# A gated-attention and two-MLP kernel: phase rounded by an int32 write, first weights decoded in x's buffers, SyncE's first transfers in a fixed order, a new plan of steps, last stores split

## The chip, the cores and the metric

The kernel runs on one core of one Trainium2 chip. The metric is device time in microseconds (us) from the start to the end of one execution; less is better. The profile's span, from the first to the last instruction, is a little shorter than that time.

## What is computed

Attention with a complex decay per step, then two MLPs over 3072 tokens (4 batches of 768) with 384 features and 2048 hidden units, all in float32:

```python
mag = sqrt(a_re**2 + a_im**2); scale = minimum(mag, 0.999) / (mag + 1e-6)
for t in range(S):                      # S_re, S_im: [B, H, 48, 48]
    S_re, S_im = a_t * (S_re + 1j * S_im)   # real and imaginary part, a_t scaled
    S_re += outer(k_t, v_t)
    y_t = q_t @ S_re
x = y.reshape(3072, 384)
h = x @ moe_w_in;  x = (h * clip(h + 3, 0, 6) / 6) @ moe_w_out
h = x @ moe2_w_in; out = (h * sigmoid(1.702 * h)) @ moe2_w_out
```

## The kernel before

The recurrence is done in 24 chunks of 128 steps. A preparation block covers 256 tokens (two chunks). For each block the decays' logarithms and angles are summed along time (two scans), and q and k are multiplied by exp, cos and sin of the sums. Only block 0 is split in two halves of one chunk each; its steps carry a third number (`round.0.1` is half 1 of block 0). Rows of q and k are then put into another partition order by small transfers from SBUF to SBUF, the "repack": `repE.c`/`reqE.c` move the cos part of chunk `c` and `repS.c`/`reqS.c` the sin part; `rep` is issued by SyncE (SP) and GpSimd (POOL), `req` by ScalarE (ACT), and `req` exists in block 0 alone. One chunk of attention on TensorE (PE) is `sc` (scores), `kt` (k transposed), `pv`, `ud` (state update) and, in chunks 0 to 3, `xp`; ACT copies `ks` and `ysb`, and VectorE (DVE) does the mask `p` and the state `um`/`ua`.

The result x of a chunk is split into a high and a low part, `xh` (ACT) and `xl` (DVE), since a float32 product is made of three fast matmuls: high*high, low*high, high*low. The first MLP is cut into slots; `in.s` is the first matrix of slot s, `g1` to `g4` its gate on ACT, DVE, ACT, DVE, and `out.s` its second matrix. In the first two blocks of 512 tokens the slots `in.0` to `in.3` do tokens 0 to 255 with the weights wi0 to wi3, `in.4` to `in.7` tokens 256 to 511 with the same. Each of these is 18 matmuls of 256 columns.

The 16 weight pieces of the first MLP (even: wi, odd: wo, two of a number) come as 768 KB each of packed words. `W.i` loads one, DVE decodes it in three steps `da`, `db`, `dc`, ACT makes the high part (`hi.i`) and DVE the low part (`lo.i`). Before, the decoded words go to two buffers of a pool `st`.

The order of DVE, ACT and PE in the first MLP and the attention is written out in the string `PLAN`, a list of such steps made by a planner; each engine runs its steps in that order and waits on semaphores. SP's and POOL's order is left to the scheduler. Matmuls `wm.0` (16 of them, without use for the result) stand ahead of the first chunk. After the plan (slot 82 on) a loop over the remaining slots follows, with the second MLP.

Of the kernel before, what the change touches and what calls it, by code (L numbers as in the profile page):

```python
# [43 lines left out]
cos.0.1 qksin.0.0 reqE.0 qkcos.0.1 repS.0 reqS.0 qksin.0.1 W.5 da.3 La.1 reqE.1 repS.1 da.4 db.3 reqS.1 repE.1 db.4 kt0.0 dc.3 sc0.0 W.6 ks0.0 W.7 dc.4 tab1.1
kt1.0 sc1.0 p0.0 ks1.0 hi.3 ud.0 p1.0 lo.3 im2.1 pv0.0 um.0 pv1.0 re2.1 da.1 ysb.0 mag2.1 Lq.1 sc0.1 hi.4 W.9 kt0.1 ln.1 p0.1 sc1.1 lo.4 ks0.1 pv0.1 inv.1 p1.1
mag.1 kt1.1 db.1 pv1.1 ks1.1 half.1 eps.1 xp.0 dc.1 ysb.1 lneps.1 ud.1 da.2 lnhalf.1 decay.1 xp.1 xh.0 scan.1 invhalf.1 xh.1 tan.1 E0.1 xl.0 E1.1 xl.1 lastE.1
ua.1 lastqk.1 in.0 tab2.1 qkE.1 atan.1 um.1 in.2 hi.1 La.2 carry.1 low.1 Lv.2 angle.1 g1.0 W.11 W.10 W.12 g1.2 W.13 round.1 W.8 turns.1 frac.1 lo.1 abs.1 db.2
sin.1 cos.1 keep.1 dc.2 qkcos.1 hi.2 re2.2 tab1.2 qksin.1 repE.2 im2.2 lo.2 W.14 repS.2 g2.0 in.1 mag2.2 g3.0 g4.0 ln.2 g2.2 W.15 out.0 inv.2 Lv.4 da.8 Lv.3
g1.1 db.8 repS.3 eps.2 g2.1 dc.8 mag.2 g3.1 da.5 repE.3 half.2 hi.8 sc0.2 lneps.2 g4.1 kt0.2 g3.2 p0.2 sc1.2 ks0.2 lo.8 lnhalf.2 kt1.2 p1.2 pv0.2 ks1.2 decay.2
invhalf.2 pv1.2 g4.2 ud.2 scan.2 ysb.2 Lq.2 xp.2 ua.2 E0.2 low.2 um.2 sc0.3 xh.2 db.5 E1.2 kt0.3 sc1.3 p0.3 ks0.3 xl.2 kt1.3 lastE.2 p1.3 lastqk.2 pv0.3 ks1.3  # L50
dc.5 tab2.2 pv1.3 da.6 tan.2 ud.3 ysb.3 hi.5 db.6 xp.3 atan.2 lo.5 carry.2 out.1 dc.6 xh.3 xl.3 hi.6 da.7 angle.2 in.4 lo.6 round.2 g1.4 in.3 db.7 turns.2 dc.7
out.2 g1.3 ua.3 hi.7 g2.3 frac.2 g3.3 in.7 g4.3 abs.2 g2.4 sin.2 lo.7 cos.2 qkE.2 out.3 g3.4 g1.7 g4.4 tab1.3 in.6 qkcos.2 keep.2 repE.4 qksin.2 out.4 g1.6
g2.6 da.12 in.5 g3.6 g2.7 g4.6 g3.7 db.12 in.9 g1.5 g4.7 g2.5 dc.12 g3.5 in.8 g4.5 hi.12 um.3 g1.9 lo.12 repS.5 out.5 g1.8 da.14 da.9 db.14 repS.4 out.6 db.9
dc.14 La.3 dc.9 hi.14 repE.5 out.7 lo.14 hi.9 lo.9 g2.8 sc0.4 g2.9 g3.8 kt0.4 g3.9 p0.4 sc1.4 ks0.4 g4.8 im2.3 kt1.4 p1.4 pv0.4 ks1.4 g4.9 re2.3 pv1.4 da.10
da.11 ud.4 db.10 ysb.4 xf.4 mag2.3 sc0.5 dc.10 ln.3 sc1.5 ua.4 Lq.3 hi.10 in.12 p0.5 Lv.5 inv.3 um.4 Lv.6 mag.3 db.11 out.8 eps.3 p1.5 lo.10 g1.12 lneps.3
dc.11 in.10 da.13 hi.11 g2.12 xh.4 db.13 in.11 g1.10 lo.11 g3.12 g2.10 dc.13 g3.10 out.9 g1.11 g4.10 hi.13 g2.11 pv0.5 decay.3 g3.11 half.3 out.10 g4.11
lnhalf.3 g4.12 invhalf.3 pv1.5 lo.13 scan.3 out.11 ysb.5 xf.5 tan.3 E0.3 in.13 low.3 E1.3 xl.4 da.15 lastE.3 lastqk.3 qkE.3 tab2.3 out.12 atan.3 db.15 g1.13
in.15 La.4 angle.3 xh.5 g2.13 in.14 round.3 g3.13 turns.3 g1.15 g4.13 g1.14 frac.3 out.13 xl.5 abs.3 g2.14 sin.3 g2.15 in.16 cos.3 dc.15 keep.3 g3.14 qkcos.3
g3.15 in.17 hi.15 qksin.3 repE.6 im2.4 tab1.4 in.18 g4.14 repS.6 g1.16 g4.15 lo.15 g1.17 g1.18 clip.4 out.14 repS.7 g2.16 re2.4 g2.17 g3.16 mag2.4 out.15
# [793 lines left out]
```

## Time and profile before

| | |
|---|---|
| three runs of before | 996.52, 997.92, 1000.21 us (median 997.92) |
| profiled execution | 998.55 us, span 996.8 us |
| PE busy | 948.4 us (95% of the span), mean granted clock 0.983 |
| DVE, ACT, POOL busy | 643.9, 517.7, 105.8 us |
| chain that ended last | PE 89%, DVE 5%, ACT 2%, DMA 2% |

PE is busy in almost all of the span, and the busy share of the other engines is an average over a crowded start and a quieter rest. So what matters is the time at which PE waits, and the time that it runs at the lower of its two clocks (1.2 GHz, shown as 0.50; 1.00 is 2.4 GHz).

### The profile page before, as it was taken

The page shows a single profiled execution, that of the slowest core. Times are in us where ns is not written, and L with a number is a line of the kernel's source. Part 1 is how long each engine was busy: PE and PEld are TensorE (multiplying, and loading weights), DVE is VectorE, ACT ScalarE, POOL GpSimd, SP SyncE. Part 2 cuts the span into 40 slices and gives each one's busy share as a digit, 9 for nine tenths or more (in the row PEclk, how much of TensorE's full clock was granted, in tenths as well). Part 3 has the DMA queues.
Part 4 walks back from the last instruction along what each step waited for, and adds up shares of the span by engine and source line. Part 5 has one row for each costly group of instructions (what it writes and reads, how often), then busy time and mean ns, then how long its engine had stood idle before and what let it go on. Part 6 is the DMA issues. An engine that isn't in the chain of part 4 may idle for free.

```text
span 996.8 us, 14418 instructions
## 1 busy us (share of the span) xinstructions
PE 948.4 (95%) x5378; PEld 804.8 (81%) x5378; DVE 643.9 (65%) x919; ACT 517.7 (52%) x860; POOL 105.8 (11%) x218
## 2 busy tenths in 40 slices
...
GB/s 270 283 163 196 66 49 125 131 128 128 122 118 96 72 120 128 80 97 73 72 132 240 159 151 40 1 125 128 127 190 127 158 159 127 111 1 1 32 1 35
DMA packets 70684, 113.63 MB, mean 114 GB/s; under 512 B 9936, under 2 KB 55632, under 8 KB 70608
## 3 DMA queue, kind: packets, MB, share of 16 engines
...
q10 hardware_dynamic: 384, 0.26, 0.1%
...
## 4 chain that ended last, share of the span: by engine, by line
PE 89%; DVE 5%; ACT 2%; DMA 2%; issue 1%; SPq 0%; POOL 0%; ACTq 0%; DVEq 0%
PE h L634 38%; PE o L672 38%; PE sc L517 4%; PE ud L563 3%; PE yps L537 3%; PE yps L539 2%; PE kt L526 1%; DMA wr<-in_w1i 1%; DMA QK<-qk 1%; DVE qk L474 1%; DVE pE L473 1%; DMA xf<-ysb 0%; DVE wi L389 0%; DVE pA L436 0%; DVE wx L127 0%
## 5 line engine op out<-in xcount | busy, mean ns | idle before, releaser
L634 PE MATMUL h<-xh,wi 128*128 128x512 f32 (+1 forms) x1248 | 364.9, 376 | 10.8 <-ACT wi L380 6.4
L672 PE MATMUL o<-gh,wo 128*128 128x512 f32 (+1 forms) x1248 | 364.2, 376 | 0.1
L634 PEld LDWEIGHTS h<-xh,wi 128*128 128x128 f32 x1248 | 228.0, 190 | 52.9 <-ACT wi L380 6.6
L672 PEld LDWEIGHTS o<-gh,wo 128*128 128x128 f32 x1248 | 227.2, 189 | 41.7 <-issue 0.9
L634 PE MATMUL h<-xl,wi 128*128 128x512 f32 (+1 forms) x624 | 233.9, 375 | 0.5 <-DVE xl L606 0.4
L672 PE MATMUL o<-gl,wo 128*128 128x512 f32 (+1 forms) x624 | 233.1, 374 | 0.0
L659 DVE TENSOR_TENSOR gl<-tt,gh 128x512 fp32r<-128x512 f32 x192 | 132.2, 690 | 84.0 <-ACT gh L654 83.7
L654 ACT ACTIVATE gh<-tt 128x512 fp32r<-128x512 f32 x192 | 121.0, 632 | 109.3 <-DVE tt L649 65.2
L649 DVE TENSOR_TENSOR tt<-tt,h 128x512 f32<-128x512 f32 x96 | 66.0, 688 | 144.8 <-ACT tt L641 144.8
L641 ACT ACTIVATE tt<-h 128x512 f32<-128x512 f32 x96 | 57.4, 598 | 172.2 <-PE h L634 167.2
L634 PEld LDWEIGHTS h<-xl,wi 128*128 128x128 f32 x624 | 118.3, 190 | 22.2 <-DVE xl L606 1.2
L672 PEld LDWEIGHTS o<-gl,wo 128*128 128x128 f32 x624 | 117.8, 189 | 21.0
L639 ACT ACTIVATE tt<-h,b 128x512 f32<-128x512 f32 x96 | 65.7, 685 | 75.5 <-PE h L634 72.1
L647 DVE SCALAR_TENSOR_TENSOR tt<-tt,h 128x512 f32<-128x512 f32 x96 | 65.2, 683 | 42.4 <-ACT tt L639 42.2
L551 POOL DMA_DIRECT2D xf<-ysb x60 | 30.9, 521 | 242.0 <-ACT ysb L543 232.1
L517 PE MATMUL sc<-QK 96*128 96x128 f32 x384 | 55.0, 291 | 0.0
L517 PEld LDWEIGHTS sc<-QK 96*128 96x128 f32 x384 | 50.8, 203 | 2.2 <-issue 0.7
L486 POOL DMA_DIRECT2D QK<-pE x70 | 35.7, 515 | 157.8 <-DVE pE L473 95.9
L521 DVE TENSOR_TENSOR p<-sc,causal 128x512 f32<-128x512 f32 x48 | 33.0, 688 | 20.7 <-PE sc L517 19.7
L537 PE MATMUL yps<-p,v 128*48 128x128 f32 (+1 forms) x384 | 40.4, 291 | 0.1
L486 POOL DMA_DIRECT2D QK<-qk x70 | 36.4, 526 | 15.6 <-issue 5.8
L603 ACT ACTIVATE xh<-xf 128x384 fp32r<-128x384 f32 x44 | 22.8, 518 | 27.8 <-DMA xf<-ysb 11.5
(111 smaller groups left out, 877.9 us busy)
## 6 DMA issues: line engine op xcount, KB each, us to landing
...
```

The source lines that it names most:

```text
L486: e.dma_start(out=dst, in_=src)
L517: T.matmul(out=sc[:, i, :], lhsT=kv_(4 * g + i), rhs=qv(4 * g + i), start=True, stop=True)
L521: V.tensor_tensor(out=p, in0=s_["sc", g], in1=causal.unsqueeze(1).to_broadcast([P, 4, CH]), op=ALU.mult)
L537: T.matmul(out=yps[r0:r1, h // 2, :], lhsT=v_c[c][:, e], rhs=s_["p", g][:, i, :], start=True, stop=first)
L634: T.matmul(out=h[:, i, :], lhsT=w[:, k, :], rhs=x[:, k, :], start=(k == 0 and q == 0), stop=(k == 2 and q == 2))
L639: A.activation(out=t, in_=ht[s], func=AF.Relu, bias=b3)
L641: A.activation(out=t, in_=ht[s], func=AF.Sigmoid, scale=1.702)
L647: V.scalar_tensor_tensor(out=t, in0=t, scalar=6.0, in1=ht[s], op0=ALU.min, op1=ALU.mult)
L649: V.tensor_tensor(out=t, in0=t, in1=ht[s], op=ALU.mult)
L654: A.activation(out=hi, in_=gt[s][0], func=AF.Copy)
L659: tail[:] = [V.tensor_tensor(out=lo, in0=gt[s][0], in1=gt[s][1], op=ALU.subtract)]
L672: T.matmul(out=acc[:, o:o + n], lhsT=w[:, e * P:e * P + P], rhs=g[:, i, :], start=(f == o == q == 0), stop=(f == FT - 1 and q == 2), skip_ ...
```

## The change

The diff, with most of the plan's lines left out:

```diff
-MAGIC = 12582912.0
...
 PLAN = """
...
-inv.0.1 db.0 lneps.0.0 eps.0.1 decay.0.0 mag.0.1 lneps.0.1 half.0.1 lnhalf.0.0 decay.0.1 lnhalf.0.1 scan.0.0 invhalf.0.0 invhalf.0.1 scan.0.1 E0.0.0 E1.0.0
...
+hi.1 kt1.0 W.5 dc.2 W.9 ks1.0 W.4 ysb.0 lo.1 ud.0 W.15 ln.1 lo.0 inv.1 xp.0 um.0 mag.1 eps.1 half.1 da.3 lneps.1 lnhalf.1 decay.1 reqS.1 scan.1 invhalf.1 xh.0
...
+    first_sp = {"last": None, "open": True}
+
+    def sp(**kw):
+
+        r = nc.sync.dma_start(**kw)
+        if first_sp["last"] is not None:
+            after(r, first_sp["last"])
+        if first_sp["open"]:
+            first_sp["last"] = r
...
-        nc.sync.dma_start(out=raw[i].rearrange("p n w -> p (n w)"), in_=(w1i, w1o)[kind][j].bitcast(U32))
+        sp(out=raw[i].rearrange("p n w -> p (n w)"), in_=(w1i, w1o)[kind][j].bitcast(U32))
...
         if k == 0:
-            w32[i] = st.tile([P, 768], U32, tag="ws", name="wx")
+            if i >= 4:
+                w32[i] = st.tile([P, 768], U32, tag="ws", name="wx")
+            else:
+                if i % 2 == 0:
+                    memo["wx"] = xp.tile([P, 2, 768], U32, tag=("xl", "xh")[i // 2], name="wx")
+                w32[i] = memo["wx"][:, i % 2]
...
-            o, n = (0, TB) if c is None else (c * CH, CH)
-            nc.sync.dma_start(out=ins[b, "a"].rearrange("p q j t -> p (q j) t")[:, :, o:o + n],
-                              in_=a_t[b].rearrange("p (q j t) -> p (q j) t", q=2, j=3)[:, :, o:o + n])
+            src = a_t[b].rearrange("p (q j t) -> p q j t", q=2, j=3)
+            if c is None:
+                sp(out=ins[b, "a"], in_=src)
+            else:
+                for q in (1, 0):
+                    (nc.scalar.dma_start if c == 0 and q else sp)(out=ins[b, "a"][:, q, :, c * CH:c * CH + CH], in_=src[:, q, :, c * CH:c * CH + CH])
...
-        op("round", lambda: V.tensor_scalar(out=pB(), in0=pA(), scalar1=2.0 / TURN, scalar2=MAGIC, op0=ALU.mult, op1=ALU.add))
-        op("turns", lambda: V.tensor_scalar(out=pB(), in0=pB(), scalar1=MAGIC, scalar2=None, op0=ALU.subtract))
-        op("frac", lambda: V.scalar_tensor_tensor(out=pA(), in0=pA(), scalar=2.0 / TURN, in1=pB(), op0=ALU.mult, op1=ALU.subtract))
+        whole = lambda: pB().bitcast(mybir.dt.int32)
+        op("round", lambda: V.tensor_scalar(out=whole(), in0=pA(), scalar1=2.0 / TURN, scalar2=None, op0=ALU.mult))
+        op("frac", lambda: V.scalar_tensor_tensor(out=pA(), in0=pA(), scalar=2.0 / TURN, in1=whole(), op0=ALU.mult, op1=ALU.subtract))
...
-                e = (nc.sync, nc.gpsimd, nc.scalar)[i % (3 if b == 0 else 2)]
-                if e in queues:
-                    e.dma_start(out=dst, in_=src)
+                q = "SASGGA"[i] if b == 0 else "SG"[i % 2]
+                if q in queues:
+                    {"S": sp, "G": nc.gpsimd.dma_start, "A": nc.scalar.dma_start}[q](out=dst, in_=src)
+            if c == 1 and y == 1 and "S" in queues:
+                first_sp["open"] = False
...
+        if m == 1 and b == NT // TK - 1 and e:
+            for i in range(2):
+                part = slice(i * TB, i * TB + TB)
+                if e == 1 or i:
+                    V.tensor_copy(out=y[:, part], in_=ops_["o"][e][:, part])
+                else:
+                    A.activation(out=y[:, part], in_=ops_["o"][e][:, part], func=AF.Copy)
+                (nc.sync, nc.scalar)[i].dma_start(out=out[b * 2 + i, :, e, :], in_=y[:, part])
+            return
```

So one DVE instruction (`turns`) is gone from each block; the weights 0 to 3 are decoded in two buffers that x's parts use only later; SP's transfers up to chunk 1's repack keep the order in which they are written; a chunk's repack in block 0 gives ACT one of the two large pieces (48 partitions x 774), which was POOL's; the first quarter of the decays comes through ACT's queue; and the last two output tiles are copied and stored in halves. Three places show how the plan moved the rest.

SP at the start, before. `a` are decays (142 is block 0, 274 block 1), `wr` weights, `QK_249` and `QK_276` chunks 0 and 1 of the repack:

```order
L399 DMA a_142<-in_a_t 128x6x128 x2
L412 DMA v_146<-in_v_t 128x384
L360 DMA wr_148<-in_w1i 128x1536
L406 DMA qk_150<-in_qk_t 128x3x128 x4
L412 DMA v_155<-in_v_t 128x384
L360 DMA wr_157<-in_w1o 128x1536
L360 DMA wr_159<-in_w1o 128x1536
L360 DMA wr_161<-in_w1i 128x1536
L360 DMA wr_165<-in_w1i 128x1536
L360 DMA wr_270<-in_w1o 128x1536
L486 DMA QK_249<-pE_197 48x774
L486 DMA QK_249<-pE_197 16x258
```

SP at the start, of the change, from chunk 0's weights on (chunk 1 is now `QK_281`, block 1's decays `a_220`):

```order
L326 DMA wr_159<-in_w1o 128x1536
L326 DMA v_162<-in_v_t 128x384
L326 DMA wr_164<-in_w1i 128x1536
L326 DMA v_169<-in_v_t 128x384
L326 DMA a_220<-in_a_t 128x1536
L326 DMA QK_249<-pE_196 48x774
L326 DMA QK_249<-pE_196 32x258
L326 DMA QK_249<-qk_150 48x774
L326 DMA QK_249<-qk_150 32x258
L326 DMA QK_281<-pE_196 48x774
L326 DMA QK_281<-pE_196 32x258
L326 DMA QK_281<-qk_150 48x774
```

Three weights instead of six stand ahead of the repacks, and block 1's decays, which stood between the two parts of chunk 0's repack (row 13 of SP before), now stand ahead of it too.

ACT around chunk 1's repack, before (all of it follows chunk 0's at once):

```order
L486 DMA QK_249<-qk_150 32x258 x2
L486 DMA QK_276<-pE_197 32x258 x2
L486 DMA QK_276<-qk_150 32x258 x2
L531 ACTIVATE ks_306<-kt_293 128x384
L325 ACT_TABLE_LOAD
L531 ACTIVATE ks_306<-kt_312 128x384
```

ACT at the same place, of the change:

```order
L502 DMA QK_281<-pE_196 48x774
L502 DMA QK_281<-pE_196 32x258
L549 ACTIVATE ks_317<-kt_301 128x384
L393 ACTIVATE wo0_321<-wx_167 128x768
L549 ACTIVATE ks_317<-kt_323 128x384
L561 ACTIVATE ysb_336<-yps_117 112x512
L339 ACTIVATE pB_286<-pA_269 128x768
L339 ACTIVATE pA_269<-pB_286 128x768
L339 ACTIVATE pC_360<-pB_286 128x768
L344 ACTIVATE pA_269<-pA_269,bone_109 128x768
L339 ACTIVATE pA_269<-pA_269 128x768
L339 ACTIVATE a_220<-a_220 128x768
```

Behind the last of these stands `QK_281<-qk_150 48x774`, ACT's part of chunk 1's sin repack: ten activations have moved in between ACT's cos part and its sin part.

DVE ahead of the first gate, before (`wi1_537` is the low part of the weights of `in.1`, `tt_512` the first gate):

```order
L465 SCALAR_TENSOR_TENSOR pA_351<-pA_351,pB_339 128x768
L389 TENSOR_TENSOR wo0_503<-wx_353,wo0_503 128x768
L125 SCALAR_TENSOR_TENSOR wx_436<-wr_161,wx_436 128x768
L466 TENSOR_SCALAR carry_111<-pA_351 128x3
L127 SCALAR_TENSOR_TENSOR wx_436<-wr_161,wx_436 128x768
L473 TENSOR_TENSOR pE_452<-qk_358,pB_339 128x12x128
L474 TENSOR_TENSOR qk_358<-qk_358,pC_399 128x12x128
L389 TENSOR_TENSOR wi1_537<-wx_436,wi1_537 128x768
L647 SCALAR_TENSOR_TENSOR tt_512<-tt_512,h_460 128x512
```

DVE of the change, from the two low parts of the weights to x's low part of chunk 1 (`xl_373<-xp_465`):

```order
L402 TENSOR_TENSOR wi2_443<-wx_392,wi2_443 128x768
L123 SCALAR_TENSOR_TENSOR wx_213<-wr_319,wx_213 128x768
L486 TENSOR_TENSOR qk_387<-qk_387,pE_380 128x12x128
L121 TENSOR_SCALAR wx_473<-wr_418 128x768
L123 SCALAR_TENSOR_TENSOR wx_473<-wr_418,wx_473 128x768
L477 TENSOR_TENSOR pB_286<-pB_286,carry_111 128x3
L452 SCALAR_TENSOR_TENSOR pA_269<-mask_p_107,pB_286 128x768
L480 TENSOR_SCALAR pB_286<-pA_269 128x768
L481 SCALAR_TENSOR_TENSOR pA_269<-pA_269,pB_286 128x768
L125 SCALAR_TENSOR_TENSOR wx_473<-wr_418,wx_473 128x768
L587 TENSOR_TENSOR U_124<-ud_453,U_124 96x384
L624 TENSOR_TENSOR xl_373<-xp_465,xh_372 128x3x128
```

The low parts of wi0, wi1 and wi2 now stand ahead of x's low part of chunk 1, that of wi3 five rows behind it; `in.0` to `in.3` follow each other on PE, where before `in.0`, `in.2` and `in.1` did.

## Rows read from the trace of the kernel before

**Rows 1.** Waits of PE: who waited for whom; us in total, times, longest

```profile
PE h L634 <- ACT wi L380: 6.4, 1, 6.4
```

**Rows 2.** PE's timeline: start, us, line, operation, count, idle before and releaser

```profile
22.00 6.14 PE L745 MATMUL warm<-pB,ident 128*128 128x128 f32 x32 [22.00 <-ACT pB L331]
35.09 0.88 PE L526 MATMUL kt<-ident,QK 96*128 96x96 f32 x4 [6.96 <-DMA QK<-qk]
...
44.44 2.08 PE L517 MATMUL sc<-QK 96*128 96x128 f32 x8
...
57.60 0.51 PE L634 MATMUL h<-xh,wi 128*128 128x256 f32 x2 [0.67 <-ACT xh L603]
...
72.68 0.58 PE L634 MATMUL h<-xh,wi 128*128 128x256 f32 x1 [2.88 <-DVE wi L389]
...
79.34 1.05 PE L517 MATMUL sc<-QK 96*128 96x128 f32 x8
...
97.10 0.40 PE L634 MATMUL h<-xh,wi 128*128 128x256 f32 x2
97.34 0.28 PE L634 MATMUL h<-xl,wi 128*128 128x256 f32 x1
```

**Rows 3.** One-us windows of PE: length, busy (count), granted clock, DMA share, GB/s

```profile
30.00:31.00 1.00, 0.00 (x0) 0.65 1.19 220
...
50.00:51.00 1.00, 1.00 (x10) 0.61 1.05 430
```

**Rows 4.** Windows by stage: busy us of each engine (count), clock, DMA share, GB/s

```profile
0.00:28.00 28.00, 6.00 (x32) 5.98 (x32) 19.47 (x35) 17.57 (x41) 5.92 (x23) 1.00 0.78 264
28.00:50.00 22.00, 15.04 (x89) 14.29 (x89) 10.79 (x17) 8.66 (x14) 1.63 (x4) 0.55 0.90 292
...
70.00:80.00 10.00, 7.32 (x41) 7.32 (x42) 9.29 (x12) 7.83 (x11) 6.40 (x12) 0.60 0.88 234
...
100.00:150.00 50.00, 49.63 (x376) 44.83 (x375) 49.30 (x70) 32.17 (x50) 9.09 (x17) 1.00 0.23 60
...
300.00:400.00 100.00, 99.15 (x603) 83.19 (x602) 71.38 (x100) 65.83 (x108) 24.09 (x48) 1.00 0.40 104
```

**Rows 5.** Timelines of ACT and DVE, chunk 0's second table load and sin product

```profile
15.90 1.28 ACT L325 ACT_TABLE_LOAD   x1
...
24.77 0.95 DVE L474 TENSOR_TENSOR qk<-qk,pC 128x768 f32<-128x768 f32 x1
```

**Rows 6.** Timeline of SP's queue: issues of block 1's decays and the sin repack

```profile
24.82 0.54 SPq L399 DMA_DIRECT2D a<-in_a_t  x1
...
28.12 6.49 SPq L486 DMA_DIRECT2D QK<-qk  x4
```

**Rows 7.** DMA issues, window 22 to 45, then whole span: KB, median us to landing

```profile
QK<-pE ACTq DMA_DIRECT2D x4, 32.2 KB, 6.9
...
QK<-qk SPq DMA_DIRECT2D x24, 145.1 KB, 3.5
```

**Rows 8.** Groups by line and form: count, busy us, mean ns, idle before

```profile
L331 ACT ACTIVATE pE<-pC 128x768 f32<-128x768 f32 x22 | 18.0, 840 | 2.1 <-DVE U L569 1.8 <-DVE pC L436 0.3
L531 ACT ACTIVATE ks<-kt 128x384 f32<-128x384 f32 x40 | 19.5, 488 | 27.2 <-PE kt L526 16.5 <-DMA QK<-qk 10.6
L436 DVE TENSOR_TENSOR_SCAN pA<-mask_p,pB 128x768 f32<-128x768 uint8 x11 | 19.3, 1755 | 1.1 <-ACT pB L331 1.0
L465 DVE SCALAR_TENSOR_TENSOR pA<-pA,pB 128x768 f32<-128x768 f32 x11 | 10.5, 953 | 0.1
L464 DVE TENSOR_SCALAR pB<-pB 128x768 f32<-128x768 f32 x11 | 6.1, 556 | 0.2
L125 DVE SCALAR_TENSOR_TENSOR wx<-wr,wx 128x768 uint32<-128x768 uint32 x16 | 15.1, 951 | 0.1
```

**Rows 9.** Timeline of the end: ACT's last copies, SP's last stores

```profile
988.10 1.90 ACT L676 ACTIVATE y<-o 128x512 f32<-128x512 f32 x3 [2.77 <-PE o L672]
...
988.72 1.80 SPq L681 DMA_DIRECT2D out<-y  x3
```

More of the change, by code (lines that the diff above doesn't have):

```diff
@@ L44 @@
[L44 to L59, printed above, removed]
@@ L60 @@
-repE.7 g3.17 g4.16 ln.4 g4.17 inv.4 g2.18 sc0.6 mag.4 kt0.6 p0.6 sc1.6 ks0.6 half.4 eps.4 kt1.6 pv0.6 p1.6 ks1.6 lneps.4 pv1.6 Lq.4 ud.6 ysb.6 decay.4 y0.15
-xf.6 sc0.7 lnhalf.4 um.6 sc1.7 invhalf.4 p0.7 Lv.7 g3.18 kt0.7 Lv.8 p1.7 in.19 ks0.7 scan.4 xh.6 kt1.7 tan.4 lastE.4 pv0.7 lastqk.4 ks1.7 xl.6 E0.4 pv1.7 g4.18
-E1.4 low.4 ud.7 ysb.7 qkE.4 y1.15 xf.7 y2.15 tab2.4 out.16 ua.7 um.7 atan.4 carry.4 La.5 angle.4 out.17 xh.7 g1.19 xl.7 round.4 in.21 turns.4 frac.4 g2.19
-abs.4 out.18 keep.4 clip.5 g3.19 cos.4 g4.19 in.20 sin.4 qkcos.4 g1.21 re2.5 qksin.4 out.19 g1.20 im2.5 g2.20 repS.9 in.23 g2.21 g3.20 g3.21 g4.20 tab1.5 g4.21
@@ L68 @@
-Lv.10 La.6 g4.27 repE.11 in.28 g1.26 g2.26 repS.11 g3.26 sc0.10 g1.28 g4.26 kt0.10 p0.10 sc1.10 ks0.10 clip.6 im2.6 kt1.10 pv0.10 p1.10 ks1.10 re2.6 g2.28
-pv1.10 mag2.6 ud.10 Lq.6 ysb.10 ln.6 xf.10 sc0.11 ua.10 inv.6 um.10 sc1.11 mag.6 p0.11 Lv.11 out.25 eps.6 p1.11 half.6 lneps.6 lnhalf.6 in.29 decay.6 g3.28
-scan.6 invhalf.6 out.26 g1.29 g4.28 E0.6 tan.6 E1.6 pv0.11 g2.29 lastE.6 lastqk.6 qkE.6 out.27 tab2.6 atan.6 low.6 pv1.11 g3.29 angle.6 in.30 ysb.11 xh.10
-xf.11 g4.29 round.6 out.28 xl.10 g1.30 turns.6 g2.30 frac.6 g3.30 in.31 g4.30 abs.6 keep.6 xh.11 out.29 cos.6 xl.11 sin.6 qkcos.6 g1.31 in.32 tab1.7 g2.31
@@ L84 @@
-ks0.16 half.9 g1.50 kt1.16 p1.16 out.48 ks1.16 g2.50 eps.9 g3.50 in.51 lneps.9 g4.50 lnhalf.9 decay.9 scan.9 sc0.17 g1.51 pv0.16 invhalf.9 g2.51 E0.9 pv1.16
-p0.17 g3.51 ud.16 low.9 ysb.16 g4.51 E1.9 xf.16 tan.9 sc1.17 lastE.9 lastqk.9 ua.16 tab2.9 out.49 um.16 Lv.17 p1.17 atan.9 in.52 angle.9 xh.16 round.9 pv0.17
-g1.52 xl.16 pv1.17 g2.52 turns.9 g3.52 out.50 ysb.17 g4.52 xf.17 frac.9 qkE.9 in.53 abs.9 sin.9 cos.9 keep.9 out.51 g1.53 tab1.10 g2.53 qkcos.9 in.54 g3.53
-xh.17 g4.53 repE.19 out.52 qksin.9 g1.54 g2.54 repS.19 in.55 xl.17 g3.54 g4.54 out.53 La.10 g1.55 repE.18 g2.55 g3.55 in.56 g4.55 repS.18 out.54 g1.56 im2.10
```

105 lines of the change are left out of this document (66 added, 39 removed).

## The prediction

> **What bounds the kernel now.** I read the windows by stage first. From 300 to 400 us PE is busy 99.15 of 100 us, from 100 to 150 us 49.63 of 50 [rows 4]; after the first 100 us there is almost no wait left to remove, and every step there can only add. The start is different: 0 to 28 us holds 6.00 us of PE work, 28 to 50 us holds 15.04 us at a mean clock of 0.55, and 70 to 80 us holds 7.32 us at 0.60 [rows 4]. PE's timeline says why [rows 2]. PE does nothing until 22.00, then runs 6.14 us of matmuls without use, then idles 6.96 us until 35.09 for chunk 0's repack. The clock falls to 1.2 GHz in that idle stretch (0.65 in the window 30 to 31) and comes back only at 50 to 51 (0.61) [rows 3], so chunks 0 and 1 (35.09 to 57.60) run mostly at half speed. The waits list adds 6.4 us for the weights of `in.1` from ACT [rows 1], and the timeline 2.88 us for the same weights from DVE [rows 2].
>
> So a change counts if it moves the moment at which PE starts to run without a break, about 73 us now, or if it opens a gap behind it. VectorE is the second thing to watch: from 100 to 150 us it is busy 49.30 of 50 us [rows 4], which means that work that PE does earlier must also be fed earlier by a DVE that has no slack there. Its slack lies before: from 28 to 50 us it is busy 10.79 of 22 us [rows 4], 11.2 us idle.
>
> **Chunk 0 (gain 7.1 us).** The sin product of chunk 0 ends on DVE at 24.77 + 0.95 = 25.72 [rows 5]. The change takes from its path one `turns` (0.36 us for a half block: two thirds of the 0.556 of the whole one [rows 8]) and three DVE steps of the other half that stood between its two products (about 1.7 us by half-block durations); the start of the chain stays, since it hangs on the second table load at 15.90 + 1.28 [rows 5], which the quarters of decays and ACT's queue do not move. I take 23.4. Before, SP issued block 1's 768 KB of decays at 24.82 and the sin repack only at 28.12 [rows 6], and it landed 6.9 us later; now the decays and three weights stand ahead of it, 5.1 MB in all up to the repacks. At the 264 GB/s of the first 28 us [rows 4] these are through by 19.4 us, so they are not in the way. Issue 0.6, landing 3.5 (the median of SP's sin repacks over the span [rows 7]): 23.4 + 0.6 + 3.5 = 27.5, at most 31 with the 6.9 that ACT's pieces took in this stretch [rows 7]. Without use, PE is busy until about 27.4. I take 28.0 for the first useful matmul in place of 35.09, and since the idle stretch is then under 1 us, full clock for chunk 0: from 28.0 to 35.1 (its 9.35 us from 35.09 to 44.44 [rows 2] halve to about 5.0; 1.5 us for `xp.0`, which now comes ahead, and 0.6 of waits for `ks`).
>
> **Chunk 1 (gives back most of it).** ACT's part of chunk 1's sin repack used to follow chunk 0's at once. Now ten activations lie ahead of it, among them two `ks` that wait for PE's `kt` (0.49 each) and a `ysb` that waits for `pv`; `ysb.0` ends at about 32.7, then five or six steps of 0.84 [rows 8] put the issue at 37.4 to 38.6. Landing 3.5 to 6.9 [rows 7], with weights in flight on SP: 41 to 45.5, I take 43.5, against 44.44 now [rows 2]. So PE idles 35.1 to 43.5 and the clock falls, as it did after 28.1 [rows 3]. Chunk 1 runs at half clock as before (44.44 to 57.60, 13.16 us [rows 2]): PE has it done at 56.7. `in.0` needs `xl.1` from DVE: from the scores at 45.5 on, sixteen DVE steps stand up to and with `xl.1`, 13.9 us (scan 1.755, five of 0.95, `turns` gone, the sin and cos products 1.76 [rows 8]); with 1.5 us of waiting for the scores and for the angle from ACT, 60.9. Bounds 59.4 (no wait) and 62.4 (twice that).
>
> **From `in.0` to `in.4` (gain 8.0 us).** `wi0` to `wi2` are decoded ahead of `xl.1`, since the first weights no longer wait for the two buffers of `st`; `in.0` to `in.3` then follow each other. One takes 18 matmuls at 0.36 us for three, 2.16 us [rows 2]; four, 8.6, about 2 us more while the clock is still low (0.60 at 70 to 80 [rows 4]): end at 71.5. `out.0` takes 2.1. Chunk 2 begins at 73.6 in place of 79.34 [rows 2]. From there to `in.4` the work is that of before, 79.34 to 97.10 = 17.76 us [rows 2]: 91.4. By then one more `in` is done than before at that point. Lead: 97.10 - 91.4 + 2.16 = 7.9, 8 us. Does DVE keep up? Up to there it must have done 8 us more; it had 11.2 us idle between 28 and 50 us, and three `turns` of 0.556 go. My walk through the two queues to `in.17` ends with PE at 153 to 154 us and the last first-MLP weight from DVE at 154: just in time, nothing to spare. From there on any 1 us that DVE loses up to 150 us is 1 us of the end.
>
> **The int32 write (0, up to 1.6 us lost).** Eleven `turns` of 0.556 and two halves go from DVE. No row shows a write of int32 from float32. Nearest: the one-operand form `turns` itself, 0.556, and the two-operand `frac`, 0.953 [rows 8]; by the upper end the four blocks prepared before 150 us lose 4 x 0.4 = 1.6 us, which nothing hides. `frac` reads that int32, bounded by 0.953 and its double, 3.8 us in four blocks. I take 0.556 and 0.953: the shift-and-mask decode reads and writes 32-bit integers at 0.951 with two operands [rows 8], no slower than `frac`.
>
> **Other edits.** Decoding weights 0 to 3 in the two x buffers: the first `xh` and `xl` take the other of two buffers, and the decode is over before they come round; 0, at most one `lo` (0.95) late. The order of SP costs no time on SP itself as long as a transfer ahead is ready; chunk 1's sin repack, the last of it, holds the following loads until about 38, and these weights are needed from 60 us on. The last stores: ACT's copy of the last tile ends at 990.0 and the last store is issued from 988.72 + 1.80 = 990.52 [rows 9]. Two halves, on ACT and DVE, end a copy about 0.3 sooner and are 128 KB each, but two issues of 0.6 (1.80 / 3) on ACT come behind each other: 0, within 0.5 either way.
>
> The Trainium skill, "Trainium Kernel Development and Optimization", says under its key constraints that issuing from several engines saves only issue time; by it too the split stores are worth no more than an issue, which agrees with the 0.6 here.
>
> **Sum.** 998.55 (the profiled time; span 996.8) - 8.0 = 990.5; the profiled run lies 0.6 above the median, so against that 989.9. I say 990.
>
> **Rivals.**
> *A, the clock comes back early.* If PE's work in chunk 0 at full clock and the one gap let the clock return soon after 43.5, chunk 1 takes 8 us, not 13.2, and `ysb.1`, the table load and the angle come 3 us sooner; `in.0` is then bound by DVE's 59.4 or earlier weights, and `in.0` to `in.3` run at full clock (2 us): 3.5 to 4.5 more gain, 986. Against it: in the trace the clock needed 15.5 us without a gap, 35.09 to 50.6 [rows 2, 3].
> The Trainium skill, "TensorE: Matmul & The Clock Gate", Part 1, says that the low clock is the default and that activity releases it. By that rule alone chunk 1 would speed up well before its end; the trace agrees only in direction, since 15.5 us of unbroken matmuls stood at 1.2 GHz.
>
> *B, the sin repack of chunk 1 is as slow as the slowest, or chunk 0's lands at 31.* Then PE idles over 3 us ahead of chunk 0, and the clock falls there too, or chunk 1 starts at 45.5 and all behind it is 2 to 3 us later: 992 to 993. For it: ACT's pieces took 6.9 where weights were in flight [rows 7], and four are in flight at 34 to 40 us.
>
> *C, no change.* DVE's 49.30 of 50 us [rows 4] is the bound from 100 us on: if it does not fill its idle time before, PE's lead is waited away at the gates and weights until 150 us. Loss of 4 us or more of 8, 995 to 1001. Int32 at its upper ends (1.6 + 3.8) is a part of this.
>
> *D, slower.* In the new plan eight chunks (4, 6, 10, 12, 14, 16, 18, 22) have only two matrices' work, about 4.1 us of PE, between the last part of their repack and their scores; in the old plan five had. A repack takes 3.5 us to land [rows 7] after its issue of 0.6. If this comes to x us of wait on PE for each, the gain is gone at x = 1.0, and from x = 1.6 on (13 / 8) the kernel is slower by over 0.5%: 1005 at x = 1.9. For it: 3.5 is a median; before, with five such chunks, PE waited 0.85 us in 100 [rows 4], which speaks against.
>
> **How the numbers follow.** 0.5% is 5 us, about what a measurement of this kernel can tell from no change (its three runs lie within 3.7). The forecast (987.5 to 992, by the bounds 59.4 and 62.4 of `xl.1` and 0.5 of the tail) 0.50; A 0.14; B 0.20; C 0.10; D 0.06. Faster than 993: forecast, A, and all but a little of B, 0.79; slower than 1003: 0.05; between, 0.16. Range for 8 in 10: 985 to 995, which leaves out D, most of C and the end of A.
>
> **What the profile of the changed kernel would show.** PE's first useful matmul at 28 (27.5 to 31) and clock 1.00 from there to 35; right behind it one gap of about 8 us before chunk 1's scores, released by a DMA from the sin product on ACT's queue; clock about 0.5 from 43.5; `in.0` at 61, released by DVE's `xl`; `in.0` to `in.3` without a break, chunk 2's scores at 73 to 75; no further waits. On DVE no `turns`, `round` at 0.56 and `frac` at 0.95 for 768 elements. What would make it wrong: gaps of PE between 100 and 160 us released by DVE (C), waits of about 1 us or more ahead of the scores of chunks 4 to 22 released by a DMA (D), a gap before chunk 0 above 3 us (B), a clock near 1 at 47 us (A).

## The result and the profile after

The changed kernel takes 988.57 us (median of 987.83 to 989.61), the kernel before 997.22 us on the same chip: a ratio of 0.9904 with a 95% interval of 0.9884 to 0.9924, 8.7 us less. The forecast was 990, the range 985 to 995. The profiled executions compare by their spans, 996.8 and 987.9 us. Times here are medians of 4 to 23 executions of a kernel; one execution of the run with the filled gap took 1078 us, at a mean granted clock of 0.85, and is left out of that run's ratio.

PE's waits after the change (who waited for whom; us in total, times, longest), to be held against [rows 1] and the waits in [rows 2]:

```profile
PE warm L772 <- ACT pB L339: 22.2, 1, 22.2
PE sc L535 <- DMA QK<-qk: 8.1, 2, 7.2
PE h L652 <- DVE xl L624: 1.8, 1, 1.8
PE h L652 <- ACT xh L621: 0.9, 2, 0.7
PE ud L581 <- ACT ks L549: 0.6, 1, 0.6
```

The 7.0 us for chunk 0's repack and the 6.4 and 2.9 us for the weights of `in.1` are gone. In their place stands one wait of 7.2 us for a repack, ahead of chunk 1. PE's timeline after, against [rows 2]:

```profile
28.82 2.05 PE L535 MATMUL sc<-QK 96*128 96x128 f32 x16 [0.87 <-DMA QK<-qk]
...
44.04 3.35 PE L535 MATMUL sc<-QK 96*128 96x128 f32 x14 [7.24 <-DMA QK<-qk]
...
58.91 0.80 PE L652 MATMUL h<-xh,wi 128*128 128x256 f32 x2 [0.67 <-ACT xh L621]
61.48 0.58 PE L652 MATMUL h<-xl,wi 128*128 128x256 f32 x1 [1.78 <-DVE xl L624]
...
74.65 1.05 PE L535 MATMUL sc<-QK 96*128 96x128 f32 x8
...
92.69 0.40 PE L652 MATMUL h<-xh,wi 128*128 128x256 f32 x2
```

Chunk 0 begins at 28.82 in place of 35.09, chunk 1 at 44.04 in place of 44.44: of 6.3 us, 0.4 are left. `in.0` begins later than before (58.91 against 57.60) and waits 1.78 us more for x's low part, but then four slots run without a break, where before three stood ahead of chunk 2 with waits between them, and chunk 2's scores come at 74.65 in place of 79.34. The windows by stage (length; busy us of PE, PEld, DVE, ACT, POOL; clock, DMA share, GB/s), against [rows 4]:

```profile
28.00:50.00 22.00, 13.37 (x101) 11.24 (x102) 17.48 (x24) 14.19 (x22) 1.92 (x4) 0.77 0.80 256
50.00:70.00 20.00, 17.55 (x96) 14.94 (x97) 16.48 (x21) 11.57 (x20) 3.99 (x8) 0.57 1.00 359
70.00:80.00 10.00, 9.62 (x98) 8.95 (x96) 9.81 (x15) 8.70 (x14) 1.99 (x4) 1.00 0.79 236
100.00:150.00 50.00, 50.00 (x353) 44.39 (x352) 49.90 (x68) 33.52 (x54) 8.92 (x18) 1.00 0.29 80
300.00:400.00 100.00, 99.78 (x626) 84.19 (x624) 70.16 (x101) 67.70 (x113) 24.76 (x51) 1.00 0.42 116
```

From 28 to 50 us DVE does 17.48 us of work where it did 10.79: the decoding of weights has moved into its idle time. From 100 us on PE waits less than before (50.00 of 50 and 99.78 of 100 us).

**One number for a run.** In every run below, the time from chunk 2's scores on PE to the end of the span is nearly the same: 917.3 to 918.5 us with the old plan (996.8 - 79.34 = 917.5 in the kernel before), 912.1 to 913.3 us with the new one (987.9 - 74.65 = 913.3). So the 8.9 us between the spans are 4.7 us of an earlier chunk 2 and 4.2 us of less to do or to wait for behind it (about 2.2 of these are the fourth slot, which the new plan has done by then), and among runs of one plan a run is read by the moment of its chunk 2.

### The profile page after: what moved, and what is told of

Its sections match the earlier page's. It is cut to its first block, busy times and chain, and to the rows that moved or that the text cites. A ratio compares the mean times of both kernels' runs of the same rounds, so it can differ in the third digit from the quotient of the medians.

```text
span 987.9 us, 14453 instructions
## 1 busy us (share of the span) xinstructions
PE 946.5 (96%) x5378; PEld 802.7 (81%) x5378; DVE 637.7 (65%) x909; ACT 514.4 (52%) x859; POOL 102.4 (10%) x218
## 4 chain that ended last, share of the span: by engine, by line
PE 91%; DMA 3%; DVE 3%; ACT 2%; issue 1%; SPq 0%; POOL 0%; ACTq 0%; POOLq 0%; DVEq 0%
PE h L652 39%; PE o L690 39%; PE sc L535 4%; PE ud L581 3%; PE yps L555 2%; PE yps L557 2%; DMA wr<-in_w1i 1%; PE kt L544 1%; DMA QK<-qk 1%; ACT pB L339 0%; DVE pA L452 0%; DVE pE L489 0%; DVE qk L490 0%; ACT pA L339 0%; SPq L326 0%
## 5 line engine op out<-in xcount | busy, mean ns | idle before, releaser
L535 PE MATMUL sc<-QK 96*128 96x128 f32 x384 | 52.3, 282 | 8.1 <-DMA QK<-qk 8.1
```

The costliest lines, as they stand in the source:

```text
L535: T.matmul(out=sc[:, i, :], lhsT=kv_(4 * g + i), rhs=qv(4 * g + i), start=True, stop=True)
```

## The experiments

Two questions: which part of the change makes the gain, and what holds the rest of the start. A group of runs shares its runs of the kernel before (997.3 to 997.9 us).

**Old rounding in the new plan.**

```diff
-        op("round", lambda: V.tensor_scalar(out=whole(), in0=pA(), scalar1=2.0 / TURN, scalar2=None, op0=ALU.mult))
+        def round_magic():
+            V.tensor_scalar(out=pB(), in0=pA(), scalar1=2.0 / TURN, scalar2=12582912.0, op0=ALU.mult, op1=ALU.add)
+            V.tensor_scalar(out=pB(), in0=pB(), scalar1=12582912.0, scalar2=None, op0=ALU.subtract)
+        op("round", round_magic)
```

> The changed kernel with the old rounding (two float32 operations that add and take off 12582912) inside the step round, so eleven and two halves of 0.56 and 0.36 us are back on DVE; all else as changed. Theory (the gain is made before 75 us by the earlier repack and the earlier weights, and DVE is full from 70 to 150 us): 0.36 us comes back ahead of chunk 0's scores, and 0.56 us each in the three blocks prepared up to 150 us can pass to PE: 0.5 to 2 us slower than the changed kernel, 989 to 990.5. Rival (the shorter phase is what made the gain): 5 us or more slower, 994 or above.

Measured: 990.23 us (989.71 to 991.37), ratio 0.9919 [0.9900, 0.9939]. That is 1.7 us above the changed kernel; the two ranges of single runs don't overlap, though the intervals of the ratios do. Chunk 2 comes at 76.45 (74.65), and the rest is the same (989.6 - 76.45 = 913.2): what the rounding is worth in the new plan lies wholly ahead of chunk 2. Behind it this run has ten more DVE steps of 0.56 us, and they cost nothing.

**New rounding in the old plan.** The reverse of that edit, in the kernel before: the line marked `-` above stands in for the old rounding, and `turns` is struck from the plan.

> The kernel before with the new rounding alone (one write of int32, no turns), plan and all else as before. Theory: 0.36 to 0.7 us from the path to chunk 0's repack and 0.56 us each in the blocks up to 150 us where DVE is full: 0.5 to 2 us faster than before, 995.5 to 997. Rival (the shorter phase made the gain): 990 to 993.

Measured: 989.95 us (986.47 to 993.79), ratio 0.9924 [0.9897, 0.9950]: 7.4 us faster, about as much as all the rest of the change without it. The expectation was wrong by 5 us; the single runs are wide apart (7.3 us), but all of them are below the kernel before. Eleven `turns` are 6.1 us of DVE's time, but chunk 2's scores already come at 69.69 in place of 79.34, and ahead of them stand only one whole `turns` and two halves, 1.3 us. The rows of SP's queue in this run (start, us, line, transfer):

```profile
22.93 1.25 SPq L486 DMA_DIRECT2D QK<-pE  x2
25.24 1.15 SPq L486 DMA_DIRECT2D QK<-qk  x2
28.07 0.34 SPq L399 DMA_DIRECT2D a<-in_a_t  x1
```

Before, block 1's decays stood between the two parts of chunk 0's repack (24.82), and the sin part was issued from 28.12 on [rows 6]. With the shorter step the scheduler happened to put the decays behind: the sin part goes out at 25.24. PE's timeline and the window of 28 to 50 us of the same run:

```profile
28.56 0.30 PE L526 MATMUL kt<-ident,QK 96*128 96x96 f32 x1 [0.90 <-DMA QK<-qk]
...
36.55 1.13 PE L517 MATMUL sc<-QK 96*128 96x128 f32 x8 [1.67 <-DMA QK<-pE]
...
47.12 0.50 PE L634 MATMUL h<-xh,wi 128*128 128x256 f32 x2 [0.67 <-ACT xh L603]
...
58.15 0.58 PE L634 MATMUL h<-xh,wi 128*128 128x256 f32 x1 [5.46 <-ACT wi L380]
...
69.69 1.13 PE L517 MATMUL sc<-QK 96*128 96x128 f32 x8 [1.28 <-issue]
```

```profile
28.00:50.00 22.00, 17.25 (x159) 14.19 (x160) 19.01 (x25) 16.39 (x29) 1.08 (x3) 1.00 0.86 296
```

Chunk 0 starts at 28.56, the clock stays at 1.00 up to 56 us, `in.0` starts at 47.12 in place of 57.60; the waits for `in.1`'s weights stay (5.46 and 2.9), and the clock falls in the first of them.

**The same rounding, SP held to the old order.**

```diff
+                    if c == 0 and e is nc.sync:
+                        if y == 0:
+                            memo["cos0"] = r
+                        else:
+                            after(r, memo["a1"])
...
+            if b == 1:
+                after(r, memo["cos0"])
+                memo["a1"] = r
```

> The kernel before with the new rounding alone, and besides SP is held to the order of before: cos part of chunk 0's repack, block 1's decays, sin part. Theory (SP's order made the gain): chunk 0's first matmul again at 33 to 35, end at 994.5 to 997. Rival (the shorter phase made it): as the run with the new rounding alone, 988 to 991.

Measured: 996.66 us (994.74 to 999.38), ratio 0.9982 [0.9965, 0.9999]. SP and PE of this run:

```profile
24.46 0.56 SPq L399 DMA_DIRECT2D a<-in_a_t  x1
27.73 6.57 SPq L489 DMA_DIRECT2D QK<-qk  x4
```

```profile
34.80 0.90 PE L534 MATMUL kt<-ident,QK 96*128 96x96 f32 x4 [6.73 <-DMA QK<-qk]
```

The gain is gone but for 0.7 us, which is what the int32 write is worth in the old plan as long as SP keeps the old order; with the write in both runs, SP's order makes the other 6.7 us. Chunk 0 comes 6.2 us later than in the run before (34.80 against 28.56), and both parts of this can be read on the first piece of SP's sin part: it goes out 2.5 us later (27.73 against 25.24), and it lands in 7.0 us and not in 3.3, beside the decays. The piece's issue in the run before and in this one (KB, us to landing):

```profile
QK<-qk SPq DMA_DIRECT2D x1, 145.1 KB, 3.3
...
QK<-qk SPq DMA_DIRECT2D x1, 145.1 KB, 7.0
```

**The reverse: old rounding, decays behind the sin part.** Weights 5 to 7 are held behind it too, so that they can't take the same place.

```diff
+                    if c == 0 and y == 1 and e is nc.sync:
+                        memo["sin0"] = r
...
+            if b == 1:
+                after(r, memo["sin0"])
...
+        if i in (5, 6, 7):
+            after(r, memo["sin0"])
```

> The kernel before, old rounding and all, with one thing forced on SP: block 1's decays and weights 5 to 7 (768 KB each) are issued behind chunk 0's sin repack, and not the decays ahead of it. The order of DVE, ACT and PE is that of before. Theory (the 7 us of PE's wait come from what stands on SP between the two parts of chunk 0's repack, and the new rounding alone gained only because the scheduler then put the decays behind it): chunk 0's first matmul at 28.5 to 31, end at 988 to 992. Rival (the shorter phase itself made the gain of the run with the new rounding alone): 995.5 to 997.5.

Measured: 995.18 us (993.49 to 997.05), ratio 0.9967 [0.9952, 0.9982]. Chunk 0 came where it was expected, the end did not:

```profile
30.19 0.90 PE L532 MATMUL kt<-ident,QK 96*128 96x96 f32 x4 [2.37 <-DMA QK<-qk]
...
54.85 0.51 PE L640 MATMUL h<-xh,wi 128*128 128x256 f32 x2 [0.67 <-ACT xh L609]
```

```profile
29.00:30.00 1.00, 0.00 (x0) 0.90 1.04 229
30.00:31.00 1.00, 0.81 (x5) 0.50 1.14 211
```

PE waits 2.37 us and not 0.90 and 0.63, and within that wait the clock falls to 0.50. Chunks 0 and 1 then take 24.7 us to `in.0` (30.19 to 54.85) where the run with the new rounding took 18.6 (28.56 to 47.12). So a start 1.6 us later, with the low clock behind it, came to 7.7 us at `in.0`. This isn't the SP order of the run with the new rounding alone, though. There the load of v (192 KB) came at 39.89; here the scheduler put it between the two parts:

```profile
24.61 0.61 SPq L416 DMA_DIRECT2D v<-in_v_t  x1
```

Of the 1.6 us, 0.4 are a later issue of the sin piece (25.62 against 25.24, the old rounding), and 1.2 its landing (4.5 us against 3.3). Moving the decays alone gains 2.2 us with the old rounding. Whether the place of v, the other loads or the old rounding takes the rest isn't shown.

**No fixed order on SP in the changed kernel** (`if first_sp["last"] is not None:` becomes `if False:`).

> The changed kernel without the fixed order of SP's first transfers: the scheduler puts two more weights (1.5 MB) ahead of block 1's decays and the repacks of chunk 0, and two ahead of chunk 1's; all other queues are the same. Theory: 1.5 MB at 264 GB/s is 6 us of transfers, so block 1's decays end at about 25 us and chunk 0's repack shares the DMA engines with weights and lands 1 to 3 us later; chunk 0 at 29.5 to 31, chunk 1 bound by ACT's order as now: 0 to 2 us slower than the changed kernel, 988.5 to 990.5. Rival (the fixed order is what made the gain): chunk 0 at 33 to 35 as in the kernel before, 993 or above.

Measured: 988.06 us (987.00 to 990.20), ratio 0.9901 [0.9881, 0.9922]: the same time. Here the scheduler puts block 1's decays ahead of chunk 0's cos part by itself, and chunk 0 starts at 28.69. The fixed order keeps the order from depending on chance; it makes no gain over this one. Two more weights ahead of the repacks cost nothing at chunk 0, and the expectation that they would was wrong.

**Old dealing of the repack's pieces in the changed kernel** (`"SGASGA"[i]` for `"SASGGA"[i]`, so that ACT has only small pieces).

> The changed kernel with the pieces of block 0's repack dealt out as before (SP, POOL, ACT in turn, so that ACT has no large piece and the sin part of chunk 1 no longer hangs on ACT's ten activations with 145 KB, only with two of 32 KB). Theory: ACT's two small pieces stand at the same late place, so chunk 1's scores stay at 43 to 45 and the end within 1 us of the changed kernel, 988 to 990. Rival (the large piece is what lands late): chunk 1 at 41 to 42, 987 to 988.

Measured: 987.76 us (986.95 to 989.07), ratio 0.9893 [0.9869, 0.9916]: no difference. Chunk 1 still waits, in two steps to 44.05 and 45.07, for a `QK<-qk` transfer.

**The gap ahead of chunk 1: ACT's sin part at once** (here and below, of the plan's lines only the steps around an edit are shown).

```diff
-sc1.0 p0.0 reqE.1 repS.1 kt0.0
+sc1.0 p0.0 reqE.1 reqS.1 repS.1 kt0.0
...
-lneps.1 lnhalf.1 decay.1 reqS.1 scan.1
+lneps.1 lnhalf.1 decay.1 scan.1
```

> The changed kernel with one token moved: ACT's part of chunk 1's sin repack follows its cos part at once, ahead of the ten activations. Theory: PE's gap of 7.24 us ahead of chunk 1's scores comes from those ten activations; the repack then lands at 34 to 36 in place of 44, PE has no gap over 1 us, the clock stays at 2.4 GHz through chunk 1, and chunk 1 ends 10 us or more earlier; but in.0 to in.3 then wait for the decoded weights and x's low part on DVE, and DVE has 8 us of idle time in all between 28 and 70 us, so of those 10 us at most half reach the end: 983 to 987. Rival 1 (the weights on SP hold the transfer up, not ACT's order): it lands at 41 or later, end within 1 us of the changed kernel. Rival 2 (DVE is the bound from 50 us on, nothing reaches the end): PE's gap moves to in.0 and in.1, 988 to 989.

Measured: 986.74 us (985.97 to 987.33), ratio 0.9881 [0.9860, 0.9903], 1.8 us below the changed kernel. The gap of 7.24 us is gone, but two others opened (1.52 us for a `ks` that ACT now issues late, 1.93 us for the mask `p` on DVE), and the clock fell in the first:

```profile
33.55 0.55 PE L544 MATMUL kt<-ident,QK 96*128 96x96 f32 x4 [1.52 <-ACT ks L549]
...
40.18 3.79 PE L535 MATMUL sc<-QK 96*128 96x128 f32 x16
...
46.54 0.69 PE L555 MATMUL yps<-p,v 128*64 128x128 f32 x4 [1.93 <-DVE p L539]
```

**The gap filled with matmuls without use** (a second `wm` of 20 ahead of chunk 1's scores).

> The changed kernel with 20 matmuls without use (identity by identity, 128x128 float32, about 7.2 us at full clock) ahead of chunk 1's scores, where PE now idles 7.24 us; nothing else differs. It measures what the fallen clock costs. Theory: the clock stays at 2.4 GHz, chunk 1's scores start at 44 to 44.5 as now, chunk 1 takes 8 us and not 14, in.0 is then released by DVE's low part of x at 57 to 59 in place of 61.5, in.0 to in.3 run at full clock: chunk 2's scores at 70 to 72 in place of 74.65, and the end 1 to 4 us earlier, 984.5 to 987.5, as far as DVE can follow. Rival (DVE is the bound from 50 us on): the lead is waited away before 150 us, end within 0.7 us of the changed kernel.

Measured: 989.36 us, ratio 0.9901 [0.9878, 0.9923]: the same time. The matmuls without use took 4.73 us and not the 7.2 expected, so PE still waited 3.46 us, and the clock fell in that wait. But it came back at 50 us, 17 us sooner than in the changed kernel, and chunk 1 did end early, for nothing. Two windows of PE (length, busy, clock, DMA share, GB/s) and its timeline:

```profile
43.00:44.00 1.00, 0.00 (x0) 0.64 0.89 305
50.00:51.00 1.00, 1.00 (x13) 0.95 0.81 207
```

```profile
44.52 3.36 PE L535 MATMUL sc<-QK 96*128 96x128 f32 x14 [3.46 <-DMA QK<-qk]
...
55.51 0.50 PE L652 MATMUL h<-xh,wi 128*128 128x256 f32 x2 [0.67 <-ACT xh L621]
61.28 0.58 PE L652 MATMUL h<-xl,wi 128*128 128x256 f32 x1 [5.27 <-DVE xl L624]
```

PE reaches `in.0` at 55.51 and not 58.91, and then waits 5.27 us for x's low part, which DVE gives at the same time as ever (61.28 here, 61.48 in the changed kernel). Both the expectation of a gain and the reason given for none (the lead waited away before 150 us) were wrong: it is waited away at once. What holds DVE's row stands in its timeline of the changed kernel:

```profile
45.17 0.56 DVE L121 TENSOR_SCALAR wx<-wr 128x768 uint32<-128x768 uint32 x1 [2.09 <-DMA wr<-in_w1i]
...
54.63 0.56 DVE L121 TENSOR_SCALAR wx<-wr 128x768 uint32<-128x768 uint32 x1 [1.23 <-DMA wr<-in_w1i]
...
60.89 0.54 DVE L624 TENSOR_TENSOR xl<-xp,xh 128x384 fp32r<-128x384 f32 x1
```

From 45.17, when the words of wi2 have landed, DVE works to 61.43 (eighteen instructions) with 1.2 us idle, a wait for the next weight's words. In this kernel PE's clock in chunk 1 doesn't set `in.0`; those landings and DVE's row do. Behind `in.0` the clock is at 0.50 up to 67 us in this run as in the changed kernel, so what it costs from there to chunk 2 wasn't tried.

**Four more orders of the start.** Each is an edit of the plan in the kernel ahead of it; the first is one of the changed kernel. First, ACT's sin part stands behind chunk 0's first `ks`, and weight 1's high part behind `ysb.0`:

```diff
-ks0.0 W.3 hi.1 kt1.0 W.5 dc.2 W.9 ks1.0 W.4 ysb.0 lo.1
+ks0.0 reqS.1 W.3 kt1.0 W.5 dc.2 W.9 ks1.0 W.4 ysb.0 hi.1 lo.1
...
-lneps.1 lnhalf.1 decay.1 reqS.1 scan.1
+lneps.1 lnhalf.1 decay.1 scan.1
```

> The changed kernel with ACT's part of chunk 1's sin repack behind the first ks of chunk 0 (not ahead of it as in the run before) and the high part of weight 1 behind ysb.0, so that ACT doesn't hold up chunk 0's ks. Theory: the repack lands at 36 to 37.5, PE has no gap over 1 us up to chunk 1's scores, so the clock stays at 2.4 GHz to there; but chunk 1's mask p stands on DVE behind the first step of weight 4, whose transfer lands only at 45, so PE's gap moves behind the scores (38.5 to 46.5, released by DVE) and the clock falls in it. Gain about that of the run with the sin repack at once, 986 to 988. Rival (the gap of 7.24 us is the only loss in chunk 1): in.0 at 52 to 54, 981 to 983.

Measured: 987.33 us (986.44 to 988.61), ratio 0.9894 [0.9875, 0.9913]. As expected, the gap moved behind the scores, to the mask that stands on DVE behind wi2's first step. Not as expected, the clock had fallen before them already (0.82 from 34 to 35 us), after a single wait of 1.13 us for a `ks`:

```profile
47.67 0.69 PE L555 MATMUL yps<-p,v 128*64 128x128 f32 x4 [5.03 <-DVE p L539]
...
73.34 1.05 PE L535 MATMUL sc<-QK 96*128 96x128 f32 x8
```

Then wi2 (weight 4) is loaded first, and its first step takes weight 3's place:

```diff
-reqS.1 W.3 kt1.0 W.5 dc.2 W.9 ks1.0 W.4 ysb.0
+reqS.1 W.4 kt1.0 W.3 dc.2 W.5 ks1.0 W.9 ysb.0
...
-half.1 da.3 lneps.1
+half.1 da.4 lneps.1
...
-Lq.1 da.4 db.4 E1.1 sc1.1 p0.1 kt0.1 p1.1
+Lq.1 db.4 E1.1 sc1.1 p0.1 kt0.1 p1.1 da.3
```

> The kernel of the run with ACT's part behind ks, and besides: weight 4 (wi2) is loaded ahead of weights 3, 5 and 9, its first step on DVE takes the place of weight 3's, which goes behind chunk 1's masks. Theory: DVE's wait of about 2 us for that transfer at 45 is gone, the masks of chunk 1 come at 39 to 41, chunk 1 ends on PE at 46 to 48 at full clock, and x's low part of chunk 1 is then set by DVE's work alone: 55 to 58 in place of 61.4; chunk 2's scores at 69.5 to 72 in place of 74.65, end 3 to 5 us earlier than the changed kernel: 983.5 to 985.5. Rival (DVE's 50 us from 100 to 150 us are the bound, a lead of PE is waited away there): 987 to 989, with waits of PE on DVE between 100 and 160 us.

Measured: 985.46 us (985.05 to 987.25), ratio 0.9879 [0.9860, 0.9898], 3.1 us below the changed kernel (2.5 by the ratios, whose intervals overlap) and the fastest by its median. Chunk 2 at 70.57. The clock fell in this run too (0.82 in the window 35 to 36, behind a wait of 1.05 us), so PE's chunk 1 was slower than expected. PE's timeline and the window of 100 to 150 us:

```profile
44.34 0.69 PE L555 MATMUL yps<-p,v 128*64 128x128 f32 x4 [2.89 <-DVE p L539]
...
57.54 0.58 PE L652 MATMUL h<-xl,wi 128*128 128x256 f32 x1 [1.46 <-DVE xl L624]
...
70.57 1.05 PE L535 MATMUL sc<-QK 96*128 96x128 f32 x8
```

```profile
100.00:150.00 50.00, 50.00 (x346) 44.02 (x345) 49.66 (x69) 34.82 (x56) 12.45 (x26) 1.00 0.34 93
```

To this, x's low part of chunk 1 is moved ahead of block 1's angle:

```diff
-carry.1 W.11 angle.1 round.1 frac.1 dc.6 abs.1 ua.1 sin.1 xl.1
+xl.1 carry.1 W.11 angle.1 round.1 frac.1 dc.6 abs.1 ua.1 sin.1
```

> The kernel of the run with weight 4 first, and besides x's low part of chunk 1 stands ahead of block 1's angle, round, frac and one decode step on DVE (4.4 us of work by the rows of before). Theory: in.0 then starts at 50 to 54, in.0 to in.2 run through, in.3 waits for its weights on DVE; chunk 2's scores wait for block 1's repack, which can't come earlier; chunk 2's scores at 67 to 71: 0 to 2 us gain over that run, 982 to 985. Rival (delaying the angle by 0.5 us delays block 1's repack and that sets chunk 2): same as that run or up to 1 us slower.

Measured: 987.15 us (986.36 to 987.63), ratio 0.9892 [0.9873, 0.9911]: 1.7 us worse than the run before it, the way of the rival, but more than its 1 us and not by its mechanism. `in.3` waits 2.17 us on PE for a gate on DVE, and the masks come later than in the run before it (44.73, a wait of 5.03 us, against 44.34 and 2.89).

Last, and without that move, chunk 1's masks stand ahead of block 1's first scan, and weight 1's high part ahead of `ysb.0`:

```diff
-ks1.0 W.9 ysb.0 hi.1 lo.1
+ks1.0 hi.1 W.9 ysb.0 lo.1
...
-decay.1 scan.1
+decay.1 sc0.1 sc1.1 p0.1 p1.1 scan.1
...
-E0.1 sc0.1 Lq.1 db.4 E1.1 sc1.1 p0.1 kt0.1 p1.1 da.3
+E0.1 Lq.1 db.4 E1.1 kt0.1 da.3
```

> The kernel of the run with weight 4 first (985.46), and besides chunk 1's masks stand on DVE ahead of block 1's first scan and not behind it, and the high part of weight 1 ahead of ysb.0 on ACT. Theory: PE's wait of 2.9 us for the masks goes and DVE's of 1.7 for weight 1 becomes 0.8; chunk 1 ends on PE 2 to 3 us earlier, but x's low part of chunk 1 stays at the end of DVE's unbroken row, so only the 0.9 us of DVE's idle time reach the end: 984 to 985.5. Rival (PE's wait for the masks is on the path): 982 to 983.5.

Measured: 985.99 us (984.92 to 987.38), ratio 0.9872 [0.9849, 0.9896]: no different from the run with wi2 first. The wait for the masks fell from 2.89 to 1.53 us, but a wait of 3.11 us for a `ks` on ACT took its place. x's low part sets `in.0` at 57.88 (57.54 there), though PE reached it earlier and waits 3.08 us for it:

```profile
57.88 0.58 PE L652 MATMUL h<-xl,wi 128*128 128x256 f32 x1 [3.08 <-DVE xl L624]
...
71.67 1.13 PE L535 MATMUL sc<-QK 96*128 96x128 f32 x8 [0.32 <-DMA QK<-qk]
```

**Which part makes the gain.** Of the 8.7 us the rounding makes 1.7 in the new plan; the fixed order on SP and the dealing of the pieces make nothing that these runs can tell. What is left, about 7 us, comes with the new plan and the two buffers together, which no run parts. The new rounding alone (7.4 us) and all else without it (7.7) don't add up, since each takes the decays from between the two parts of chunk 0's repack.

## Why the prediction was right, and where it was not

- **Chunk 0** (28.0, bounds 27.5 to 31): 28.82, at full clock. Right, though the sum of 27.5 was 1.2 us short: the sin product ended at 24.06 and not 23.4, and SP's large piece, issued at 24.54, landed in 4.2 us and not 3.5. Its reason, the decays between the two parts on SP, is shown in the old plan from both sides: with them between the wait is 6.73 us, behind them 2.37 or less. For the wait of the sin part before, from 25.4 to 28.1, SP's list of waits names a cos piece (issued at 24.13, landed at 28.03); why it waits for that piece only where the decays stand between isn't shown.
- **Chunk 1** (43.5, a gap of about 8 us): 44.04 after 7.24 us. Right, and ACT's ten activations are the cause: with ACT's part moved ahead of them, the gap is gone. Dealing the large piece back to POOL changes nothing.
- **Clock in chunk 1** (half): half from 40 us to 67 us. Rival A didn't come. Its price for chunk 1 was wrong as well: in the run with the filled gap the clock was back at 50 us and PE reached `in.0` 3.4 us sooner, and no time was gained, since DVE sets `in.0`. Its price for `in.0` to `in.3` at full clock no run tests.
- **`in.0` on `xl.1`** (60.9, bounds 59.4 to 62.4): 61.43. Right, in part by luck: the sum starts the row of DVE at 45.5 with chunk 1's scores, and what started it, at 45.17, was the landing of wi2's words.
- **Chunk 2** (73.6): 74.65. One us short: four slots ran to 72.49 and not to 71.5, half of it the later start, half the low clock up to 67 us. `in.4` came at 92.69 and not 91.4, so the lead there was 97.10 - 92.69 + 2.16 = 6.6 us and not 7.9.
- **The sum.** 8.9 us by the spans against 8.0: the term of the start was 1.3 us too large (6.6 and not 7.9), and 2.3 us came behind `in.4`, where the prediction had nothing. That the two misses nearly cancel is luck. PE's idle time from 100 to 150 and from 300 to 400 us went from 0.37 and 0.85 us to 0 and 0.22, 1.0 us of these; the rest isn't assigned to a row.
- **The int32 write** (0.556, bound 0.953): 0.56 for 768 elements and 0.36 for half, `frac` 0.96 with an int32 operand, as the rows of DVE after the change show:

```profile
19.59 0.36 DVE L480 TENSOR_SCALAR pB<-pA 128x384 int32<-128x384 f32 x1
...
58.08 0.56 DVE L480 TENSOR_SCALAR pB<-pA 128x768 int32<-128x768 f32 x1
58.67 0.96 DVE L481 SCALAR_TENSOR_TENSOR pA<-pA,pB 128x768 f32<-128x768 f32 x1
```

- **DVE as the coming bound** (any us it loses up to 150 us is one of the end; rival C): this step failed. DVE is full from 100 to 150 us in every run of the new plan (49.66 of 50 us and more), and still each us by which chunk 2 came earlier reached the end, down to 70.57: PE was busy 50.00 of 50 us from 100 to 150 in that run. Nor did the ten steps that the old rounding adds to DVE behind chunk 2 lengthen the run (913.2 us from there to the end, 913.3 without them). A busy share of 99% on DVE was read as a bound, though PE didn't wait for it there.
- **Rival D** (a wait ahead of eight chunks): the waits list has two waits for a repack in the whole run, 8.1 us together, both in chunks 0 and 1. It didn't come.
- **Tail** (0 within 0.5): from PE's last matmul to the end of the span 7.4 us before (988.97 + 0.39 to 996.8) and 7.5 after (980.02 + 0.39 to 987.9). Right; the last rows after the change are

```profile
980.02 0.39 PE L690 MATMUL o<-gl,wo 128*128 128x512 f32 x1
...
980.55 1.10 ACTq L701 DMA_DIRECT2D out<-y  x2
980.86 0.42 DVE L698 COPY y<-o 128x256 f32<-128x256 f32 x1 [0.34 <-ACT y L700]
```

Not tried alone: the two buffers of x for the first weights, since the new plan decodes a third weight before the first is free. That the waits of 6.4 and 2.9 us for `in.1`'s weights went with the new plan and these buffers together is shown by the runs that keep the old plan (5.5 to 6.7 and 2.9 us in all three); which of the two did it is not. The split of the last stores wasn't tried alone either.
